# Attention beside a long convolution on one core: the score banks regrouped into a ring of six, with narrower convolution chunks and more probability slots

## The chip, the core and the metric

The kernel runs on one core of a Trainium2 chip. The metric is the device time of one execution in microseconds (us); before the change it is 903.99 us, the median of five runs (902.03 to 904.02). The engines are named as the profile names them: PE (TensorE, matmuls; PEld is its weight loads), ACT (ScalarE), DVE (VectorE), POOL (GpSimd) and SP (the queue that issues most DMAs). PSUM, into which PE writes and from which ACT and DVE read, has eight banks of 128 partitions x 512 fp32 numbers.

## What is computed

Two independent operators on 2048 positions and 640 channels, whose results stand side by side in the output. Shortened:

```python
# A: gated long convolution, one filter of 2048 taps for each channel
k_shift = sum(k_pad[:, t:t+S] * shift_k[:, 3-t] for t in range(4))
kv = k_shift * v
y  = irfft(rfft(kv, 2S) * rfft(ssm_k, 2S))[:S]      # causal convolution
a  = q * (y + kv * ssm_D)
# B: attention, 32 heads of 20 channels, no mask
q, k, v = split(x @ wqkv)
p = softmax(q @ k.T * 20**-0.5)                      # 32 x 2048 x 2048
b = (p @ v) @ wo
out = concat([a, b], -1)
```

The exponentials of B are 32 x 2048 x 2048 numbers. The convolution of A is done without an FFT, by matmuls with Toeplitz blocks of the filters.

## The kernel before, in words

**Attention.** Queries are taken in 4 chunks of 512 (qc), heads in 8 groups of 4 (g), keys in 16 blocks of 128 (kb): 512 blocks. A block has four *units*, one for each head: scores of 128 keys x 512 queries, which fill one PSUM bank. There are 2048 units. `S_task` (L209, matmul at L567) writes the scores of a group of units, one unit to a bank; `EXP_task` (L579, instruction at L584) lets ACT take the exponential of two or three neighbouring banks in one instruction and write them as bf16 into slots of `P_sb`; `PV_task` (matmul at L645) multiplies the four probability tiles of a block by V and sums them over the 16 key blocks in bank 6. V carries a column of ones, so that the softmax denominators come out of the same matmul.

**Exponentials on VectorE.** Some units are given to DVE: `VEXP_task` (L589) and `vexp_iter` do the exponential in five instructions (L614, L617, L619, L622, L624), of which only the first reads the bank. `vec_at` (L1061) decides whether a unit goes there. It refuses while two such units are in work, while DVE's planned work reaches more than 0.4 us past the present (L1063), while none of 4 slots (`NPV`) is free, while the preparation or the output steps of A are behind their pace (L1067 to L1071), and while the convolution has done fewer tiles than 40 x (n - 480) / 1488 at unit n (L1072).

**Banks.** After the first units, the groups alternate between three units in banks 0 to 2 and two units in banks 3 and 4 (`group`, L188). Bank 5 (`AUX`) takes the units for DVE and the side tasks, bank 6 the output of PV, bank 7 (`MISC`) the convolution.

**Side tasks** go through `mbank` (L354), which gives them bank 5 while the convolution runs: K and Q projections of 512 positions (`KQ_task`, matmul at L393, cast at L381), V projections (L448, L454), normalisation of finished heads (`N_task`, L669 to L677), transposes of the normalised output (L702) and the output projection (L719), each evacuated by DVE.

**Operator A.** `kv_iter` (L474) makes kv on DVE (L477, L507) and writes it and four shifted copies to DRAM. Then `conv_setup` and `conv_iter` (L847) run 40 tiles of 16 channels; each has 128 matmuls (L868) into bank 7, two DVE steps on the result (L881, L882), four more matmuls (L889) and one DVE cast (L895). The shifted kv comes in chunks of `CH` = 128 channels (`kvx_load`, 4 DMAs for each chunk), the filters in 160 sets of four DMAs, four sets ahead. After each chunk `A_iter` (L906) loads q and kv, does 12 DVE steps of 128 x 4 x CH (L912) and stores.

**Order.** Nothing is scheduled by hardware or compiler: a planner in the kernel (L1077 to L1166) builds the program in order. It keeps an estimated time for each engine, and at each step issues, by preference: a score group whose banks are free; a side task whose due time is near; PV of two blocks; a piece of convolution that fits into the time until ACT would run dry; a side task that is not yet due; or a pair of matmuls on zeros (`zeros`, L318) that keeps PE at work. DVE's steps of a unit go ahead of those of A (`dve_step`, L1006). All engines run their lists in order, with waits on semaphores. Loads of filters, loads and stores of A are all in SP's one list.

The parts of one SBUF region R are used first for loading and for kv, then for the convolution.

Of the kernel before, what the change touches and what calls it, by code (L numbers as in the profile page):

```python
# [24 lines left out]
NHK = 4  # L25
CH = 128
NPA, NPV = 25, 4
NPU = NPA + NPV
NQS = 9
NU = NB * 4  # L30
NPAIR = 40
KVPACE, CONV0, CONVE = 0.9, 480, 40

# [180 lines left out]
def build_kernel(nc, A_q, A_k, A_v, A_shift_k, A_ssm_k, A_ssm_D, B_x, B_wqkv, B_wo, out):  # L214
# [3 lines left out]
    with ExitStack() as es:  # L218
# [29 lines left out]

        HK_E, KVX_E, Y_E, AST_E = HKW, 64 * CH, 16 * CH, 4 * CH
        ph0 = NCC * 2 * D + 4 * 4 * D + 2 * 5 * D + 2 * KS * D + D + 2 * D  # L250
        ph1 = NHK * HK_E + 2 * KVX_E + 2 * Y_E + 4 * AST_E
# [12 lines left out]
        kst = [carve(5 * D).rearrange("p (j d) -> p j d", j=5) for _ in range(2)]  # L264
        Ctile = carve(KS * D).rearrange("p (j d) -> p j d", j=KS)
        tA = carve(D)
        tB = carve(KS * D).rearrange("p (j d) -> p j d", j=KS)
        kvst = [carve(D) for _ in range(2)]
# [11 lines left out]
        bkb = [Buf() for _ in range(8)]  # L280
        AUX, OBANK, MISC = 5, 6, 7

        kext = nc.dram_tensor("kext_scratch", (D, KXL), BF16).ap()
# [70 lines left out]
        def mbank():  # L354
            return min(mbanks(), key=lambda i: P.ready("pe", (), [bkb[i]]))

        def mbanks():
            return [AUX] + [MISC] * (not conv_on[0]) + [OBANK] * (pv[0] == 0) + [4] * (nu[0] < NPAIR - 4)

        pv, nu, conv_on = [0], [0], [0]  # L360

# [23 lines left out]

        def KQ_mm(which, g, bk, x0, n):
            off = g * 4 * DH
            Wt = WQ if which == "Q" else WKV

            def pe(e):  # L390
                for cc in range(NCC):
                    for i in range(4):
                        ins = e.matmul(bank[bk][32 * i:32 * i + DH, 0:n],  # L393
                                       Wt[:, cc, off + i * DH:off + (i + 1) * DH], xT[:, cc, x0:x0 + n],
                                       start=(cc == 0), stop=(cc == NCC - 1), tile_position=(0, 32 * i))
                return ins
            P.op("pe", pe, reads=b_xT[x0 // 128:(x0 + n + 127) // 128] + [b_W(g, which)], writes=[bkb[bk]],
                 c=0.02 + 1.08 * n / 512, st=1.06 * n / 512, kind="col")
# [30 lines left out]
        def qs(qc, g):  # L429
            return (qc * NG + g) % NQS  # L430

        def KQ_task(which, g, c):
# [41 lines left out]
        def kv_iter():  # L474
# [4 lines left out]
            for i in range(2):  # L479

                yield [RB(b_xst[2 + i])]
                assert all(("X", t) in done for t in range(8, NKB))
                b_KM.append(Buf(b_xst[2 + i]))
                P.op("dve", lambda e, i=i: e.memset(KM[i], 0.0), writes=[b_KM[i]], c=0.8)
# [30 lines left out]
        def setup_pool():  # L515
            P.op("pool", lambda e: e.memset(V_sb[:, :, :, DH:DH + 1], 1.0), writes=[b_ones])
            P.op("pool", lambda e: e.memset(kst[0][0:KS - 1, 0:KS, :], 0.0), writes=[b_kst[0]])
            P.op("pool", lambda e: e.memset(tB[:, 0, :], 0.0), writes=[b_tB])
            P.dma("sp", kst[1][:, 0:4, :], ap(A_shift_k, [[0, 128], [1, KS * D]]), d_sk, writes=[b_kst[1]])
            P.op("pool", lambda e: e.dma_start(  # L520
                ap(kext, [[5 * KXL, 128], [KXL, 5], [1, KPAD]]),
                ap(tB, [list(tB.ap[0]), [KPAD, 5], [1, KPAD]])), reads=[b_tB], writes=[b_kext], dsem=d_kext,
                extra=[t_x3])
            P.op("pool", lambda e: e.dma_start(
                ap(kext, [[KXL, D], [1, S]], KPAD), ap(A_ssm_k, [[S, D], [1, S]])), writes=[b_kext], dsem=d_kext, kb=2560)
            P.dma("sp", Wo_sb, ap(B_wo, [[D, 128], [128 * D, NCC], [1, D]]), d_small, writes=[b_Wo])
            P.dma("sp", Dbc, ap(A_ssm_D, [[0, 128], [1, D]]), d_small, writes=[b_D])
            kst_load(0)
# [9 lines left out]

        def group():

            n = nu[0]
            k, b0 = (2, 2 * (flip[0] % 2)) if n < NPAIR else (2, 3) if flip[0] % 2 else (3, 0)
            if n == NPAIR:
                rank[0] += -rank[0] % 5
            if rank[0] % NPA + k > NPA:
                rank[0] += 1
            return n, min(k, NU - n), b0
# [8 lines left out]
        def S_bufs(n, banks):  # L556
            rd = []
            for i in range(n, n + len(banks)):
                qc, g, kb = qgk(i // 4)
                rd += [x for x in (b_KT[(g, kb // 4)], b_QT[qs(qc, g)]) if x not in rd]  # L560
            return rd, [bkb[b] for b in banks]
# [253 lines left out]
        def conv_setup():  # L815
            xw = [b_WK0, b_Wa, b_Wb] + b_x0
            allx = xw + b_xst + b_KM + b_kst + [b_C, b_tA, b_tB] + b_kvst
            cv["HK"] = [Buf(*xw) for _ in range(NHK)]
            cv["KVX"] = [[Buf(*allx) for _ in range(4)] for _ in range(2)]
            cv["Y"] = [Buf(*allx) for _ in range(2)]  # L820
            cv["Aq"] = [Buf(*allx) for _ in range(2)]
            cv["Akv"] = [Buf(*allx) for _ in range(2)]
            cv["Z"] = [Buf(), Buf()]
            hk_load(0)
            for X in range(4):
                kvx_load(0, X)
            for qd in range(1, NHK):
                hk_load(qd)
# [113 lines left out]
        def deps(key):  # L942
            k = key[0]
            if k in "KQ":
                return [("X", t) for t in range(4 * key[2], 4 * key[2] + 4)]
            if k == "V":
                return [("X", key[1])]
            if k == "T":
                return [("O", key[1] - 1, key[2], hf) for hf in range(2)] if key[1] else []
            if k == "O":  # L950
                return [("T", key[1], key[2])]
            if k == "N" and key[2] == 0 and key[1]:
                return [("T", key[1] - 1, qt) for qt in range(4)]
            return []
# [12 lines left out]
        def reads_of(key):  # L967
            k = key[0]
            if k == "X":
                return [b_x(key[1])]  # L970
            if k in "KQ":
                return b_xT[4 * key[2]:4 * key[2] + 4] + [b_W(key[1], k)] + (
                    [RB(b_QT[qs(key[2], key[1])])] if k == "Q" else [])
            if k == "V":
# [11 lines left out]
        for g in range(NG):  # L986
# [4 lines left out]
            for qc in range(1, 4):  # L991
                add(128 * qc + 16 * g - 30, 1.24, ("Q", g, qc), lambda g=g, qc=qc: KQ_task("Q", g, qc),
                    (128 * qc + 16 * g - 16 * NQS + 16) * 4)
        for kb in range(NKB):
# [44 lines left out]
        def pick(limit, slack, now, bnow):  # L1039

            mg = 0.08 if bnow < 24 else -0.1
            free = min(P.ready("pe", (), [bkb[i]]) for i in mbanks()) <= now + mg
            for ent in sorted(pend):
                if ent[0] > limit:
                    return None
                if not free or ent[5] > nu[0] or any(k not in done for k in deps(ent[3])):
                    continue
                if ent[2] > slack and ent[0] > bnow + 2:
                    continue
                if P.ready("pe", reads_of(ent[3])) <= now + 0.08:  # L1050
                    return ent
            return None

        def pv_ready(b, now):
# [6 lines left out]
        def vec_at(n, now):  # L1061

            if len(chain) > 1 or not 140 < n < NU - 30 or P.T["dve"] > now + 0.4:  # L1063
                return False
            if owner[NPA + vn[0] % NPV] // 4 >= pv[0] or any(k not in done for k in S_needs(n, 1)):
                return False
            if not kv_over:  # L1067
                if kv_done[0] < (now - 60) * KVPACE:
                    return False
            elif micro and kv_done[0] < a_at[0] + 12 * (now - a_at[1]) / (20 if conv_over else 60):  # L1070
                return False  # L1071
            elif not conv_over and conv_b < 40 * (n - CONV0) / (NU - CONVE - CONV0):  # L1072
                return False
            rd, wr = S_bufs(n, [AUX])
            return P.ready("pe", rd, wr) <= now + 0.03

        while nu[0] < NU or pv[0] < NB - 1:  # L1077
# [10 lines left out]
            if nu[0] < NU:  # L1088
                n, k, b0 = group()
                while max(owner[rank[0] % NPA:rank[0] % NPA + k]) // 4 >= pv[0]:  # L1090
# [8 lines left out]
                if not need and P.ready("pe", rd, wr) <= now + 0.03:  # L1099
                    vec = vec_at(n + k, now)  # L1100
                    S_task(n, banks)
                    EXP_task(n, k, b0)
                    if vec:
                        S_task(n + k, [AUX])
                        VEXP_task(n + k, AUX)
                    exp_end.append(P.T["act"])
                    continue
# [6 lines left out]

            ent = pick(bnow + 6, slack, now, bnow)
            if ent:
# [39 lines left out]
            if sum(x[1] for x in P.stream) < 2.1 and slack > 0.45 and bnow > 1:  # L1156
# [3 lines left out]
                if P.ready("pe", (), [bkb[OBANK]]) <= now - 0.1:  # L1160
                    zeros(OBANK, 2, True)
                    continue
                if not tail[0] and P.ready("pe", (), [bkb[AUX]]) <= now - 0.1:
                    zeros(AUX, 2, True)
                    continue
# [79 lines left out]
```

## Time and profile before

| what | us |
|---|---|
| median of 5 runs | 903.99 |
| profiled execution, its own time | 904.02 |
| its span, first to last instruction | 902.2 |
| ACT busy | 883.3 |
| PE busy, ends modelled | 866.6 |
| DVE busy | 606.3 |
| POOL busy | 51.6 |
| convolution matmuls (L868), first to last | about 230 to 855 |

The share of the span that an engine is busy does not say that it sets the time: PE's matmuls overlap each other, and their ends are modelled. The chain that ended last says which work the end waited for. An instruction's duration is from its start to its end; where an engine starts the next one before the last has ended, the durations add up to more than the engine's busy time. "Idle before" is how long an engine had nothing to do just before an instruction, and the releaser is what ended that. Windows give the same for a stretch of the span.

### The profile page before, as it was taken

The numbers are of one execution on the slowest core, as the hardware profiler recorded it, in microseconds if no ns is written. First come the engines' busy times: TensorE is split into PE (matmuls) and PEld (weight loads), VectorE is DVE, ScalarE is ACT, GpSimd is POOL, SyncE is SP. The second block draws the span as 40 slices with busy tenths as digits, with TensorE's granted clock in tenths as the row PEclk, the third lists the DMA queues.
The fourth block names the chain that finished last, engine by engine and source line by source line (L and its number), as shares of the span: only waits on it lengthen the run. The fifth ranks groups of instructions, "written<-read, shape, count | busy, mean of one in ns | idle before, by whom it ended". The sixth has DMA issues, their size and how long they took to land.

```text
span 902.2 us, 26133 instructions
## 1 busy us (share of the span) xinstructions
PE 866.6 (96%) x11614; PEld 405.6 (45%) x11614; DVE 606.3 (67%) x1101; ACT 883.3 (98%) x789; POOL 51.6 (6%) x75
## 2 busy tenths in 40 slices
PE   9999999999999999999999999999999999999997
PEld 4433322222455544545455444544444555455422
DVE  3477776676667677776775777775676675776751
ACT  6999999999999999999999999999999999999996
POOL 3002133321000000000000000000000000000000
PEclk9999999999999999999999999999999999999899
DMA  9525367757767555887546967455884657664311
GB/s 295 163 71 158 95 202 235 208 135 162 186 165 199 159 156 126 192 195 186 151 121 183 209 164 195 127 152 134 204 222 122 168 140 191 177 182 138 82 42 35
DMA packets 131740, 144.97 MB, mean 161 GB/s; under 512 B 94993, under 2 KB 106379, under 8 KB 131627
## 3 DMA queue, kind: packets, MB, share of 16 engines
q1 hardware_dynamic: 120251, 129.60, 54.0%
q0 software_dynamic: 9920, 13.33, 5.6%
q8 instruction: 91, 1.49, 0.7%
q10 hardware_dynamic: 1456, 0.37, 0.2%
q14 instruction: 22, 0.18, 0.1%
HBM read 124.67 MB, written 21.09 MB: 162 GB/s over the span
## 4 chain that ended last, share of the span: by engine, by line
ACT 94%; PE 6%; DVE 0%; issue 0%; DVEq 0%
ACT P_sb L584 94%; PE PS L567 1%; PE PS L393 1%; PE PS L318 1%; PE PS L645 1%; PE PS L448 1%; PE PS L748 0%; PE PS L369 0%; PE PS L868 0%; DVE P_sb L792 0%; DVE OT_sb L654 0%; DVEq L1181 0%; PE PS L771 0%; PE PS L669 0%; DVE KT L381 0%
## 5 line engine op out<-in xcount | busy, mean ns | idle before, releaser
L584 ACT ACTIVATE P_sb<-PS 128x1024 bf16<-128x1024 f32 (+2 forms) x781 | 878.8, 1424 | 4.5 <-PE PS L567 4.3
L567 PE MATMUL PS<-QT,KT 20*128 20x512 bf16 x2048 | 304.4, 385 | 27.0 <-ACT P_sb L584 21.5
L868 PE MATMUL PS<-R 128*128 128x128 bf16 (+15 forms) x5120 | 250.4, 193 | 1.7 <-DVE R L895 1.7
L868 PEld LDWEIGHTS PS<-R 128*128 128x128 bf16 x5120 | 199.5, 96 | 106.1 <-issue 105.9
L567 PEld LDWEIGHTS PS<-QT,KT 20*128 20x128 bf16 x2048 | 74.8, 91 | 220.3 <-ACT P_sb L584 167.6
L645 PE MATMUL PS<-P_sb,V_sb 128*21 128x512 bf16 x2048 | 158.5, 384 | 1.5 <-DVE P_sb L624 1.2
L614 DVE TENSOR_SCALAR XI<-PS 128x512 int32<-128x512 f32 x107 | 74.0, 691 | 99.5 <-PE PS L567 99.5
L617 DVE SCALAR_TENSOR_TENSOR XZ<-XI 128x512 f32<-128x512 uint16 x107 | 73.8, 689 | 2.7
L624 DVE SCALAR_TENSOR_TENSOR P_sb<-XZ,XI 128x512 uint16<-128x512 f32 x107 | 73.6, 687 | 2.1
L619 DVE SCALAR_TENSOR_TENSOR XZ<-XZ,XI 128x512 f32<-128x512 f32 x107 | 73.5, 687 | 2.0
L318 PE MATMUL PS<-Zt 128*128 128x512 bf16 x230 | 69.3, 396 | 1.0 <-DVE Zt L312 1.0
L477 DVE TENSOR_TENSOR R<-R 128x640 bf16<-128x640 bf16 (+1 forms) x96 | 57.7, 601 | 1.6
L645 PEld LDWEIGHTS PS<-P_sb,V_sb 128*21 128x21 bf16 x2048 | 31.2, 89 | 58.9 <-issue 46.4
L654 DVE CAST OT_sb<-PS 128x512 bf16<-128x512 f32 x32 | 22.1, 690 | 45.4 <-PE PS L645 45.1
L192 POOL DMA_DIRECT2D kvm_scratch<-R x64 | 43.8, 690 | 139.9 <-DVE R L507 134.6
L622 DVE TENSOR_SCALAR XI<-XI 128x512 int16<-128x512 int16 x107 | 49.1, 459 | 2.5
L393 PE MATMUL PS<-xT,R 128*20 128x512 bf16 (+2 forms) x660 | 40.4, 374 | 0.0
L381 DVE CAST KT<-PS 128x512 bf16<-128x512 f32 (+1 forms) x32 | 21.7, 677 | 27.8 <-PE PS L393 27.8
L393 PE MATMUL PS<-xT,WQ 128*20 128x512 bf16 (+1 forms) x660 | 40.3, 374 | 0.0
L381 DVE CAST QT<-PS 128x512 bf16<-128x512 f32 (+1 forms) x32 | 21.9, 683 | 21.6 <-PE PS L393 21.6
L895 DVE CAST R<-PS 128x256 bf16<-128x256 f32 x40 | 17.0, 424 | 20.0 <-PE PS L889 18.7
L454 DVE CAST V_sb<-PS 128x160 bf16<-128x160 f32 (+1 forms) x48 | 18.3, 382 | 17.6 <-PE PS L448 17.1
(51 smaller groups left out, 352.4 us busy)
## 6 DMA issues: line engine op xcount, KB each, us to landing
R<-kext_scratch SPq DMA_DIRECT2D x640, 132.0 KB, 3.0
kvm_scratch<-R POOLq DMA_DIRECT2D x64, 160.0 KB, 5.3
R<-kvm_scratch SPq DMA_DIRECT2D x20, 512.0 KB, 5.5
R<-in_A_k_dram SPq DMA_DIRECT2D x15, 640.0 KB, 3.8
kext_scratch<-in_A_ssm_k_dram POOLq DMA_DIRECT2D x1, 2560.0 KB, 13.5
R<-in_A_v_dram SPq DMA_DIRECT2D x16, 160.0 KB, 4.2
kv_scratch<-R SPq DMA_DIRECT2D x16, 160.0 KB, 4.5
R<-in_A_q_dram SPq DMA_DIRECT2D x20, 128.0 KB, 2.6
```

The costliest lines, as they stand in the source:

```text
L318: P.op("pe", lambda e: e.matmul(bank[bk], Zt, zrhs, start=start, stop=start, skip_group_check=True), reads=[b_Zt], writes=[bkb[bk]], tok=s ...
L393: ins = e.matmul(bank[bk][32 * i:32 * i + DH, 0:n], Wt[:, cc, off + i * DH:off + (i + 1) * DH], xT[:, cc, x0:x0 + n], start=(cc == 0), sto ...
L477: P.op("dve", lambda e: e.tensor_tensor(o, a, b, op), reads=reads, writes=writes, c=c)
L567: ins = e.matmul(bank[b], KT[32 * u:32 * u + DH, g, kb * 128:(kb + 1) * 128], QT[32 * u:32 * u + DH, qs(qc, g), :], start=True, stop=True, ...
L584: P.op("act", lambda e: e.activation(P_sb[:, s0:s0 + k, :], PS[:, b0 * 512:(b0 + k) * 512].rearrange("p (u q) -> p u q", u=k), ACT.Exp, sc ...
L614: step(lambda e: e.tensor_scalar(XI, bank[bk], scale * 1.4426950408889634 * w, 127.0 * w, op0=ALU.mult, op1=ALU.add), [bkb[bk]], [bi])
L617: step(lambda e: e.scalar_tensor_tensor(XZ, u, w * c2 / c3, u, op0=ALU.add, op1=ALU.mult), [bi], [bz])
L619: step(lambda e: e.scalar_tensor_tensor(XZ, XZ, w * w * c1 / c3, u, op0=ALU.add, op1=ALU.mult), [bi, bz], [bz])
L622: step(lambda e: e.tensor_scalar(hi, hi, 128.0, None, op0=ALU.mult), [bi], [bi])
L624: step(lambda e: e.scalar_tensor_tensor(P_sb[:, slot[n], :].bitcast(U16), XZ, 128.0 * c3 / w ** 3, hi, op0=ALU.mult, op1=ALU.add), [bi, bz ...
L645: ins = e.matmul(bank[OBANK][32 * u:32 * u + DH + 1, :], V_sb[:, kb, 4 * g + u, :], P_sb[:, slot[4 * b + u], :], start=(kb == 0), stop=(kb ...
L868: P.op("pe", lambda e, o=o, lhsT=lhsT, rhs=rhs, st=st, last=last: e.matmul(o, lhsT, rhs, start=st, stop=last, skip_group_check=True), read ...
```

## The change

The six banks 0 to 5 become one ring of two groups of three, once the convolution runs. The third bank of a group (2 or 5) can be left out of the group and *lent* to a side task that is due within `SIDE` = 8 blocks, or its unit can go to DVE in place of ACT; then ACT takes two banks in that group. Before the convolution begins and in the last 40 units the old grouping (three and two) stays. The unit for DVE is now the third of its own group, where it had been one more unit in bank 5.

`vec_at` refuses only when DVE's planned work reaches 0.8 us past the present, where it was 0.4. The pace of `A_iter` for its refusals is 12 steps in 50 us, where it was 60. Q projections for the query chunks 1 to 3 become two halves of 256 positions into the two halves of one bank, which is held in between, with one cast. A chunk has 80 channels in place of 128, so there are 8 chunks in place of 5, with 5 tiles in each. There are 35 slots of P for ACT in place of 25; their room comes from the narrower chunk buffers and from putting two buffers of `kv_iter` (`Ctile`, `tB`) where the input x was staged.

The core of the diff:

```diff
-CH = 128
-NPA, NPV = 25, 4
+CH = 80
+NPA, NPV = 35, 4
+SIDE = 8
...
-        Ctile = carve(KS * D).rearrange("p (j d) -> p j d", j=KS)
+        Ctile, tB = xst[0], xst[1]
...
+        THIRD = (2, 5)
...
         def mbank():
-            return min(mbanks(), key=lambda i: P.ready("pe", (), [bkb[i]]))
+            bk = min(mbanks() or [i for i in THIRD if i not in held], key=lambda i: P.ready("pe", (), [bkb[i]]))
+            if bk == lent[0]:
+                lent[0] = 0
+            return bk
         def mbanks():
-            return [AUX] + [MISC] * (not conv_on[0]) + [OBANK] * (pv[0] == 0) + [4] * (nu[0] < NPAIR - 4)
+            if conv_on[0]:
+                return [lent[0]] if lent[0] else []
+            return [AUX] * (AUX not in held) + [MISC] * (MISC not in held) + [OBANK] * (pv[0] == 0) + [4] * (nu[0] < NPAIR - 4)
...
+        def Q_part(g, c, i):
+            if i == 0:
+                q_bank[(g, c)] = bk = mbank()
+                held.add(bk)
+                KQ_mm("Q", g, bk, c * 512, 256)
+            else:
+                bk = q_bank[(g, c)]
+                held.discard(bk)
+                KQ_mm("Q", g, bk, c * 512 + 256, 256, 256)
+                copy("dve", QT[:, qs(c, g), :], bank[bk], bkb[bk], b_QT[qs(c, g)], 0.7)
...
-        def group():
+        def group(now):
             n = nu[0]
-            k, b0 = (2, 2 * (flip[0] % 2)) if n < NPAIR else (2, 3) if flip[0] % 2 else (3, 0)
+            k, b0 = (2, 2 * (flip[0] % 2)) if n < NPAIR else (3, 3 * (flip[0] % 2))
+            if k == 3 and (b0 + 2 == lent[0] or b0 + 2 in held or b0 == 3 and (not conv_on[0] or n > NU - 40) or
+                           P.ready("pe", (), [bkb[b0 + 2]]) > now + 0.03):
+                k = 2
...
-            if len(chain) > 1 or not 140 < n < NU - 30 or P.T["dve"] > now + 0.4:
+            if len(chain) > 1 or not 140 < n < NU - 30 or P.T["dve"] > now + 0.8:
                 return False
...
-            elif micro and kv_done[0] < a_at[0] + 12 * (now - a_at[1]) / (20 if conv_over else 60):
+            elif micro and kv_done[0] < a_at[0] + 12 * (now - a_at[1]) / (20 if conv_over else 50):
...
-                    vec = vec_at(n + k, now)
-                    S_task(n, banks)
-                    EXP_task(n, k, b0)
-                    if vec:
-                        S_task(n + k, [AUX])
-                        VEXP_task(n + k, AUX)
+                    if conv_on[0]:
+                        if k == 3 and not lent[0] and side_due(bnow, now):
+                            k, lent[0] = 2, b0 + 2
+                        vec = k == 3 and vec_at(n + 2, now)
+                        S_task(n, banks[:k])
+                        EXP_task(n, k - vec, b0)
+                        if vec:
+                            VEXP_task(n + 2, b0 + 2)
+                    else:
+                        vec = vec_at(n + k, now)
+                        S_task(n, banks)
+                        EXP_task(n, k, b0)
+                        if vec:
+                            S_task(n + k, [AUX])
+                            VEXP_task(n + k, AUX)
```

`side_due` looks for a waiting side task, other than a second half of Q, that is due within 8 blocks and whose inputs will be there within 0.5 us. While a bank is lent or held, the planner looks at all waiting side tasks, and no longer only at those due within 6 blocks.

## The prediction

> **What bounds it now.** The page's busy shares and its chain that ended last were read first.
>
> ```profile
> PE 866.6 (96%) x11614; PEld 405.6 (45%) x11614; DVE 606.3 (67%) x1101; ACT 883.3 (98%) x789; POOL 51.6 (6%) x75
> ...
> ACT 94%; PE 6%; DVE 0%; issue 0%; DVEq 0%
> ```
>
> ACT is busy for 98% of the span and carries 94% of the chain; PE's 6% lies in the first 40 us and at the end. So the time goes down by what is taken from ACT, as long as nothing makes ACT wait. Next, ACT's groups of instructions with their shapes kept apart:
>
> ```profile
> L584 ACT ACTIVATE P_sb<-PS 128x1536 bf16<-128x1536 f32 x380 | 626.1, 1648 | 3.0 <-PE PS L567 2.8
> L584 ACT ACTIVATE P_sb<-PS 128x1024 bf16<-128x1024 f32 x400 | 482.7, 1212 | 1.5 <-PE PS L567 1.4
> ```
>
> ACT hardly idles (4.5 us). Its two prices follow. One bank: 1648 - 1212 = 436 ns. The two rows add to 1108.8 us, but the page has L584 busy for 878.8 us, so instructions overlap. The 781 instructions took 3 x 380 + 2 x 400 + 1 = 1941 banks; 1941 x 0.436 = 846.3 us, and the other 32.5 us are 0.042 us for each instruction. The remaining 107 of the 2048 units were done by DVE. **So one more unit on DVE is worth 0.436 us, one instruction less 0.042 us.**
>
> How many more can DVE take? The convolution stretch, 230 to 855 us, first as a window (PE, PEld, DVE, ACT, POOL, clock, DMA share), then its DVE groups:
>
> ```profile
> 230.00:855.00 625.00, 608.25 (x8946) 316.19 (x8943) 437.45 (x791) 624.71 (x554) 0.00 (x0) 1.00 0.64 165
> ```
>
> ```profile
> L614 DVE TENSOR_SCALAR XI<-PS 128x512 int32<-128x512 f32 x101 | 69.8, 691 | 94.7 <-PE PS L567 94.7
> L624 DVE SCALAR_TENSOR_TENSOR P_sb<-XZ,XI 128x512 uint16<-128x512 f32 x101 | 69.4, 687 | 1.9
> L617 DVE SCALAR_TENSOR_TENSOR XZ<-XI 128x512 f32<-128x512 uint16 x100 | 69.0, 690 | 2.6
> L619 DVE SCALAR_TENSOR_TENSOR XZ<-XZ,XI 128x512 f32<-128x512 f32 x100 | 68.7, 687 | 1.9
> L622 DVE TENSOR_SCALAR XI<-XI 128x512 int16<-128x512 int16 x100 | 45.9, 459 | 2.3
> L881 DVE CAST ZH<-PS 128x256 bf16<-128x256 f32 x40 | 16.8, 419 | 8.1 <-PE PS L868 7.8
> ...
> L895 DVE CAST R<-PS 128x256 bf16<-128x256 f32 x39 | 16.5, 424 | 16.7 <-PE PS L889 15.4
> ...
> L912 DVE TENSOR_TENSOR R<-R 128x512 bf16<-128x512 bf16 x32 | 13.5, 422 | 0.7
> ```
>
> 101 of the 107 units lie here. A unit is five steps: 69.8 + 69.4 + 69.0 + 68.7 + 45.9 = 322.8 us, or 3.2 us each. DVE is idle for 625 - 437.5 = 187.5 us, and half of it, 94.7 us, stands before L614, waiting for score matmuls: 0.94 us at each unit. The refusal at 0.4 us (L1063) explains it: a unit is admitted only when DVE is nearly dry, and its scores take PE at least one score matmul more.
>
> **The change, part by part.** *Admission at 0.8 us.* DVE then still has up to one step (0.69 us) to do while the scores are made. From below, none of the 94.7 us is saved; from above, all of it, 94.7 / 3.2 = 30 units. I take three quarters, 71 us, because the row names this one wait at every unit, while other work must be lined up for it to close.
>
> *Eight chunks for five.* Before, 48 steps L912 lie in the stretch (32 of the row shown, 16 with Dbc). After, seven chunks in place of four end in it: 84 steps. Were a step still 0.42 us, that is 15 us more; if it shrinks along the line between the 128x512 and the 128x640 tensor-tensor rows (423 and 488 ns), a 320-wide step is 0.33 us and the cost 7 us. To this come three more starts of `A_iter`, in which new units are refused until loads land (the 6.7 us that DVE waited for kv_scratch fell on 3 occasions; I allow 2 us each). I take 11 + 6 = 17 us, nearer the middle as neither width is in the trace. So 71 - 17 = 54 us, 17 units. Outside the stretch I add one (205 to 230 us: DVE idle 8 of 25 us). **18 units x 0.436 = 7.8 us.** Bounds: -21 / 3.2 = -7 units in the stretch if nothing of the wait is saved and chunks cost 15 + 6 us, +30 - 2 = +28 with all of it and 7 us.
>
> *Groups of three.* Before, the stretch has 554 ACT instructions of 2.5 banks, 1385. After, 1385 - 17 = 1368 banks. Groups of two are those with a DVE unit (118) and those that lend a bank. Side tasks in the stretch, by their evacuations: 18 Q, 23 head normalisations, 12 transposes, 24 projections, 77; each shortens one or two groups, since the bank comes back only after DVE's cast, and I take 1.3, 100 groups. Then 218 groups of two take 436 banks, (1368 - 436) / 3 = 311 of three the rest: 529, 25 less. **25 x 0.042 = 1.0 us** (1.4 us at one group each, 0.3 us at two). [...]
>
> [...]
>
> *Score matmuls and PE.* A lent bank or a DVE unit adds no score matmul. Q in halves makes 40 matmuls for 20: halves of 256 appear as 40 in 1.3 us against 20 of 512 in 1.19 us, +0.1 us on 18 tiles. PE hides it: between 250 and 850 us it waited 91 us for ACT to free score banks (81.7 in its weight loads, 9.3 in matmuls), besides its matmuls on zeros. If that cover were gone it would cost 2 us.
>
> *A new wait.* Score matmuls into banks 2 and 5 now also wait for DVE's reading of a unit or a side task. Queued behind them on PE are PV and convolution; ACT waits for the group. The planner takes two banks if the third is not due free, so it arises only where DVE runs later than planned; the cover is the group ACT is in, 1.3 us (3 x 0.436 + 0.042), longer than a DVE step. Zero, at most one 0.69 us step at a few tens of units, some 10 us, which the upper end takes in with the slower rival.
>
> *DMA.* Rows of 160 B for 256 B, the same bytes: chunk loads go from 20 x 2048 to 32 x 2048 packets, loads and stores of A from 60 x 512 to 96 x 512, 43,000 more. Between 550 and 600 us, without a chunk change, DMAs are 54% busy at 141 GB/s; between 500 and 550 us, with one, 78% at 187. So 0.24 x 50 us x 16 engines for 8192 chunk packets and a few of A, some 23 ns each; 43,000 of them are 62 us of all 16 engines, and the stretch goes from 64% to about 74%. The sets for four quads ahead hide that: nothing. The packets of one chunk change are as many as before, so its peak is no higher.
>
> [...]
>
> *35 slots, shared buffers.* More slots let PV lag, and take no instruction away: nothing. `Ctile` and `tB` wait for the first x tiles' transposes, which come before those that the same step waited for already; SP's and POOL's lists keep their order there: nothing. SP's list grows by 12 chunk loads and 36 transfers of A; its long waits in 250 to 850 us are for PE to free filter sets (183 us), so issuing has room.
>
> Sum: 904.02 (span 902.2, and 1.8 around it; the runs' median is 903.99) - 7.8 - 1.0 = **895.2 us**.
>
> **The rivals.** *Unit count unchanged.* The other refusals (A's pace, two units in work) take over from 0.4 us. For it: DVE also waits for many short things beside L614. Only the groups remain: 904 - 1 = 903.0 us.
>
> *Slower: the convolution's own pace.* The stretch does 1385 + 101 = 1486 units in 40 tiles, 37.2 units a tile, exactly the pace of L1072 (1488 / 40). A DVE that is always full makes the two returns in each tile, L881 and L895, wait; before they found it idle (8.1 and 16.7 us). One step of 0.69 us at each is 2 x 0.69 x 40 = 55 us. If PE cannot use its windows meanwhile, tiles fall behind and L1072 refuses units until DVE is emptier by those 55 us: 17 fewer than before, 904 + 7.4 - 1.0 = 910.4 us. It decides as soon as a tile lasts over 37.2 units. Against it: PE waits for ACT 91 us in that stretch and could catch up, and longer groups give longer windows.
>
> *More.* The whole wait closes, and part of DVE's other 93 us of idle time: +40 units, 904 - 17.4 - 1 = 885.6 us.
>
> **How the numbers follow.** Chances: forecast 0.55, unchanged 0.13, slower 0.2, more 0.12. A run can tell about 0.2%, 1.8 us, from no change. Faster: 0.55 + 0.12 and a little of the unchanged case, 0.70; same 0.10; slower 0.20. The range reaches from just below the case of more, 885, to near the slower one, 908; the bounds of the forecast itself, 890 (28 + 1 units, 1.4 us) to 906 (7 - 1 lost, 0.3 us), lie inside.
>
> **What would show it.** Right: about 125 instructions at L614, the idle time before each well under 0.5 us, DVE busy over 70% in the stretch, some 750 instructions at L584 with the 1536-wide the majority in the stretch, and ACT's idle time still about 5 us. Wrong: L614 at 107 or less, or L868 reaching past 880 us (pace); ACT idle by tens of us before L584 with PE waiting for DVE at L567 (the new wait); PE waiting for R<-kvm_scratch (DMA).

## The result, and the profile after

The change runs at **902.09 us** (median of 53 runs, 900.83 to 908.0) against 903.94 us for the kernel before (95 runs, 901.24 to 919.01): a ratio of 0.9976, 95% interval 0.9966 to 0.9986. Ratios, here and below, leave out the few runs that were more than 1.5% above the fastest of their kernel; medians do not. The change is faster, but by 0.24% where I had forecast 1%. The 895.2 us are 7 us away; the rival "unit count unchanged", 903.0 us, is nearest. The profiled execution of after took 907.72 us (span 905.9), more than most of its runs. A *dip* explains that, a stretch in which the granted clock of TensorE is 0.50; it lies at 230 us and is shown below.

The page of after, first busy shares, then the granted clock in 40 slices, then the chain:

```profile
PE 873.2 (96%) x12174; PEld 422.3 (47%) x12174; DVE 605.2 (67%) x1127; ACT 883.7 (98%) x761; POOL 51.6 (6%) x75
...
PEclk9999999999699999999999999999999999999999
...
ACT 89%; PE 7%; DMA 2%; DVE 1%; SPq 0%; issue 0%; POOL 0%; POOLq 0%; DVEq 0%
```

ACT sets the end as before, and DVE is no busier (605.2 us, was 606.3). ACT's groups by shape, now at L610:

```profile
L610 ACT ACTIVATE P_sb<-PS 128x1536 bf16<-128x1536 f32 x437 | 643.5, 1639 | 6.2 <-PE PS L593 5.9
L610 ACT ACTIVATE P_sb<-PS 128x1024 bf16<-128x1024 f32 x316 | 350.3, 1201 | 2.6 <-PE PS L593 2.5
```

437 and 316 are 753 instructions where there were 781. They took 3 x 437 + 2 x 316 = 1943 banks, so DVE did 2048 - 1943 = 105 units. Before it did 107. The groups came out as forecast; the units did not: 18 more were forecast, and two fewer came.

The convolution stretch, 230 to 860 us as it now lies (PE, PEld, DVE, ACT, POOL, clock, DMA share, GB/s), and DVE's groups in it:

```profile
230.00:860.00 630.00, 615.68 (x9211) 324.94 (x9208) 428.35 (x801) 625.05 (x526) 0.00 (x0) 0.99 0.70 164
```

```profile
L640 DVE TENSOR_SCALAR XI<-PS 128x512 int32<-128x512 f32 x96 | 66.3, 690 | 55.0 <-PE PS L593 54.0
...
L938 DVE TENSOR_TENSOR R<-R 128x320 bf16<-128x320 bf16 x56 | 18.0, 322 | 1.3
...
L921 DVE CAST R<-PS 128x256 bf16<-128x256 f32 x38 | 16.1, 424 | 23.8 <-PE PS L915 23.5
L907 DVE CAST ZH<-PS 128x256 bf16<-128x256 f32 x38 | 16.1, 423 | 43.6 <-PE PS L894 43.5
...
L740 DVE CAST Bout<-PS 128x320 bf16<-128x320 f32 x24 | 11.8, 491 | 23.2 <-PE PS L745 23.2
L388 DVE CAST QT<-PS 128x512 bf16<-128x512 f32 x17 | 11.8, 691 | 21.8 <-PE PS L400 21.6
```

L640 is the old L614, and the wait before it did shrink: 55.0 us for 96 units, 0.57 us each, where it was 94.7 for 101, 0.94 each. **But DVE is idle for 630 - 428.35 = 201.7 us, more than the 187.5 before.** The 40 us that closed there reappeared at other rows: the cast of a convolution tile (L907) waits 43.6 us where it waited 8.1, the output projection's cast (L740) 23.2 for 6.7, the Q cast (L388) 21.8 for 10.6. A wait in an in-order list is closed only if the list gets something else to do at that point; here it did not.

### The profile page after: what moved, and what is told of

Read it like the earlier page. It is cut to its first block, busy times and chain, and to the rows that moved or that the text cites. A ratio compares the mean times of both kernels' runs of the same rounds, so it can differ in the third digit from the quotient of the medians.

```text
span 905.9 us, 27478 instructions
## 1 busy us (share of the span) xinstructions
PE 873.2 (96%) x12174; PEld 422.3 (47%) x12174; DVE 605.2 (67%) x1127; ACT 883.7 (98%) x761; POOL 51.6 (6%) x75
## 4 chain that ended last, share of the span: by engine, by line
ACT 89%; PE 7%; DMA 2%; DVE 1%; SPq 0%; issue 0%; POOL 0%; POOLq 0%; DVEq 0%
ACT P_sb L610 89%; PE PS L593 2%; PE PS L400 1%; PE PS L671 1%; PE PS L894 1%; DMA kvm_scratch<-R 1%; DMA R<-kvm_scratch 1%; PE PS L319 1%; PE PS L774 0%; DVE R L498 0%; SPq L193 0%; PE PS L469 0%; PE PS L376 0%; POOL kvm_scratch L193 0%; DVE P_sb L818 0%
## 5 line engine op out<-in xcount | busy, mean ns | idle before, releaser
L610 ACT ACTIVATE P_sb<-PS 128x1536 bf16<-128x1536 f32 (+1 forms) x753 | 879.2, 1455 | 8.7 <-PE PS L593 8.3
L593 PE MATMUL PS<-QT,KT 20*128 20x512 bf16 x2048 | 294.2, 387 | 23.8 <-ACT P_sb L610 18.5
L894 PE MATMUL PS<-R 128*128 128x128 bf16 (+15 forms) x5120 | 252.5, 194 | 3.1 <-DMA R<-kvm_scratch 1.7
L894 PEld LDWEIGHTS PS<-R 128*128 128x128 bf16 x5120 | 202.7, 97 | 105.0 <-issue 103.8
L593 PEld LDWEIGHTS PS<-QT,KT 20*128 20x128 bf16 x2048 | 72.5, 91 | 210.2 <-ACT P_sb L610 163.4
L640 DVE TENSOR_SCALAR XI<-PS 128x512 int32<-128x512 f32 x105 | 72.5, 690 | 61.4 <-PE PS L593 60.4
L319 PE MATMUL PS<-Zt 128*128 128x512 bf16 x310 | 91.1, 388 | 1.5 <-DVE Zt L313 1.0
L650 DVE SCALAR_TENSOR_TENSOR P_sb<-XZ,XI 128x512 uint16<-128x512 f32 x105 | 72.3, 689 | 2.4
L907 DVE CAST ZH<-PS 128x256 bf16<-128x256 f32 x40 | 16.9, 423 | 43.7 <-PE PS L894 43.5
L400 PE MATMUL PS<-xT,WQ 128*20 128x256 bf16 (+1 forms) x1140 | 43.2, 287 | 0.0
L388 DVE CAST QT<-PS 128x512 bf16<-128x512 f32 (+1 forms) x32 | 21.9, 683 | 31.8 <-PE PS L400 31.5
L388 DVE CAST KT<-PS 128x512 bf16<-128x512 f32 (+1 forms) x32 | 21.7, 677 | 24.8 <-PE PS L400 24.6
L319 PEld LDWEIGHTS PS<-Zt 128*128 128x128 bf16 x310 | 21.0, 98 | 28.8 <-issue 22.0
```

The source lines that it names most:

```text
L319: P.op("pe", lambda e: e.matmul(bank[bk], Zt, zrhs, start=start, stop=start, skip_group_check=True), reads=[b_Zt], writes=[bkb[bk]], tok=s ...
L400: ins = e.matmul(bank[bk][32 * i:32 * i + DH, o:o + n], Wt[:, cc, off + i * DH:off + (i + 1) * DH], xT[:, cc, x0:x0 + n], start=(cc == 0), ...
L593: ins = e.matmul(bank[b], KT[32 * u:32 * u + DH, g, kb * 128:(kb + 1) * 128], QT[32 * u:32 * u + DH, qs(qc, g), :], start=True, stop=True, ...
L610: P.op("act", lambda e: e.activation(P_sb[:, s0:s0 + k, :], PS[:, b0 * 512:(b0 + k) * 512].rearrange("p (u q) -> p u q", u=k), ACT.Exp, sc ...
L640: step(lambda e: e.tensor_scalar(XI, bank[bk], scale * 1.4426950408889634 * w, 127.0 * w, op0=ALU.mult, op1=ALU.add), [bkb[bk]], [bi])
L650: step(lambda e: e.scalar_tensor_tensor(P_sb[:, slot[n], :].bitcast(U16), XZ, 128.0 * c3 / w ** 3, hi, op0=ALU.mult, op1=ALU.add), [bi, bz ...
```

## The experiments

"Units" below are the instructions of DVE's first step, out of 2048. The table has every kernel; the text takes them by question. Ratios are to the kernel before, measured beside each batch (its median was 902.29 us beside e1 to e4, 903.70 beside e5 to e8, 904.04 beside e9 to e12), with 95% intervals.

| kernel | median us | ratio | units |
|---|---|---|---|
| e1, before with 0.8 | 915.35 | 1.0091 (1.0057 to 1.0126) | 118 |
| e2, e1 with 80 channels | 912.42 | 1.0122 (1.0090 to 1.0154) | 113 |
| e3, after without the ring | 918.04 | 1.0161 (1.0128 to 1.0195) | 109 |
| e4, after with 25 slots | 925.60 | 1.0245 (1.0208 to 1.0283) | 104 |
| e5, e3 with filling zeros | 904.90 | 1.0001 (0.9975 to 1.0027) | 109 |
| e6, e5 with pace 300 | 945.05 | 1.0458 (1.0429 to 1.0487) | 120 |
| e7, e6 with 0.6 and whole Q | 942.03 | 1.0430 (1.0396 to 1.0464) | 122 |
| e8, after with 0.4 | 907.60 | 1.0047 (1.0018 to 1.0076) | 97 |
| e9, after with filling zeros | 904.00 | 0.9981 (0.9953 to 1.0009) | 105 |
| e10, e9 with all of A's loads ahead, pace 100, 0.6 | 899.72 | 0.9926 (0.9897 to 0.9955) | 113 |
| e11, e10 without the ring, whole Q | 899.64 | 0.9938 (0.9910 to 0.9965) | 116 |
| e12, after with 0.85 | 913.17 | 1.0080 (1.0045 to 1.0115) | 108 |

### One part alone: the admission, then the chunks

Theory: the later admission alone gives units, and other parts of the change take them back. Rival: the refusals beside it leave it none.

```diff
-P.T["dve"] > now + 0.4:
+P.T["dve"] > now + 0.8:
```

> The kernel before with only the admission at 0.8 us. Its list holds 118 DVE units, 11 more than before. The forecast's own theory (a unit is worth 0.436 us and nothing else changes): 11 x 0.436 = 4.8 us less, 899.2 us, ACT idle time still about 5 us, idle time before the first step of a unit well under 0.94 us each. The theory of a second limit (the units are there, but PE then runs late with scores or convolution): idle time before the unit's first step falls too, ACT idle time rises by about as much as the units take away, time within 3 us of before.

e2 is the same with `CH = 80`.

> The run before it, with chunks of 80 channels in addition. Its list holds 113 DVE units. If eight output stages cost DVE what the prediction said (17 us, 5 units): 5 x 0.436 = 2.2 us more than the run before it. If narrow rows hurt by DMA instead: PE waits for R<-kvm_scratch and convolution matmuls come later, 5 us or more.

e1 has 118 units, 11 more than before, and e2 113: the narrower chunks cost five, as I had priced them. **Both are slower all the same**, e1 by 0.9% where 11 x 0.436 = 4.8 us should have been won. The wait per unit did shrink, to 71.7 / 108 = 0.66 us, and in all by 94.7 - 71.7 = 23.0 us, which at 3.2 us are the 7 units more in this stretch (108 for 101). Three views of e1 show it and what took the gain: DVE's first step in 230 to 860 us, the PE timeline (start, length, line, idle before it and releaser), and three windows:

```profile
L614 DVE TENSOR_SCALAR XI<-PS 128x512 int32<-128x512 f32 x108 | 74.7, 692 | 71.7 <-PE PS L567 69.1
```

```profile
688.35 0.40 PE L645 MATMUL PS<-P_sb,V_sb 128*21 128x512 bf16 x4 [1.90 <-DVE P_sb L624]
```

```profile
680.00:690.00 10.00, 7.96 (x102) 3.91 (x102) 7.26 (x15) 9.08 (x9) 0.00 (x0) 1.00 0.72 169
690.00:702.00 12.00, 12.00 (x139) 6.77 (x127) 7.97 (x13) 8.89 (x8) 0.00 (x0) 0.50 0.34 91
702.00:710.00 8.00, 8.00 (x94) 3.66 (x92) 2.96 (x6) 7.30 (x7) 0.00 (x0) 0.90 0.47 137
```

A unit admitted while DVE still has 0.8 us to do is also finished later, and PV, which PE does in order, stands until it is there. Such waits of PE for L624 were 1.2 us in four places before; in e1 they are 10.7 us in eleven. After one of 1.90 us the granted clock drops to 0.50, until 703.7 us. PE is then busy for all of the 12 us shown, and ACT, fed at half speed, for 8.89 of them. The profile has two more such dips, of 3.4 us, at 232 and 253 us, after waits of 1.90 and 1.59 us for L624. ACT's waits for scores are 9.9 us where they were 4.3.

### The ring, and the dip at the start of the convolution

Theory: the ring is worth its 25 instructions, 1 us. Rival: it carries more, or costs units. e3 is after with the ring switched off (`RING = 0`: groups of three and two, bank 5 for side tasks and units); halves, slots, chunks and both planner numbers stay.

```diff
+RING = 0
...
+            if k == 3 and b0 == 3 and not RING:
+                k = 2
...
-                    if conv_on[0]:
+                    if RING and conv_on[0]:
```

> The changed kernel with the ring of six switched off: groups of three and two in banks 0 to 4, bank 5 for side tasks and DVE units, as before; the wide admission, 80 channels, 35 slots, Q in halves and the pace of 50 us stay. Its list holds 109 DVE units and 780 exp instructions where the changed kernel has 105 and 753. If the ring is where the change earns its time (prediction: 25 instructions less, 1 us): 1 us slower than the changed kernel or the same. If the ring itself costs DVE units and convolution time: the convolution ends tens of us earlier than in the changed kernel, and the time is equal or better.

It is 16 us slower than after, with 109 units, four more. The PE timeline at the start of the convolution and the windows around it:

```profile
227.26 0.39 PE L596 MATMUL PS<-QT,KT 20*128 20x512 bf16 x3
231.71 1.01 PE L897 MATMUL PS<-R 128*128 128x128 bf16 x9 [4.06 <-DMA R<-kvm_scratch]
```

```profile
225.00:231.00 6.00, 2.13 (x14) 0.60 (x13) 3.12 (x5) 4.46 (x4) 0.00 (x0) 1.00 1.05 167
231.00:240.00 9.00, 8.29 (x85) 4.24 (x85) 3.85 (x6) 4.39 (x4) 0.00 (x0) 0.51 0.81 196
240.00:260.00 20.00, 20.00 (x216) 9.71 (x220) 8.15 (x14) 13.94 (x12) 0.00 (x0) 0.50 0.44 103
```

PE stands 4.06 us for the first filters' kv, and the clock is 0.50 until 269 us. ACT is busy 22.8 of these 35 us. So e3 doesn't measure the ring. e5 is e3 with 14 matmuls on zeros ahead of the first convolution matmul, so that PE doesn't stand:

```diff
+if conv_b == 0 and 0 < pv[0] % NKB:
+    for _ in range(14):
+        P.op("pe", lambda e: e.matmul(bank[OBANK], Zt, zrhs, start=False, stop=False, skip_group_check=True),
+             reads=[b_Zt], writes=[bkb[OBANK]], tok=False, c=0.0, kind=P.kind)
```

> The kernel of the no-ring run with 14 matmuls on zeros put into PE's list just before the first convolution matmul, everything else in the same order. In the no-ring run PE stood 4.1 us for R<-kvm_scratch there and the granted clock was 0.50 from 231 to over 264 us while ACT waited. If the standing PE is what lowers the clock and the lower clock is what costs the time: no stretch at 0.50 near 230 us, ACT's idle time before exp down by 10 us or more, time 902 to 906 us. If the late data itself costs it: clock the same or not, time still 910 us or more.

```profile
225.00:231.00 6.00, 5.48 (x36) 2.35 (x32) 3.13 (x5) 4.31 (x4) 0.00 (x0) 1.00 1.18 212
231.00:240.00 9.00, 9.00 (x152) 4.88 (x150) 6.55 (x11) 8.31 (x8) 0.00 (x0) 1.00 0.71 178
240.00:260.00 20.00, 19.48 (x320) 10.64 (x318) 14.91 (x28) 20.00 (x19) 0.00 (x0) 1.00 0.61 155
```

The dip is gone in the profile, all 12 runs have a mean clock of 0.999 or 1.0, and the time falls from 918.04 to 904.9 us with the same work and units. **The dip cost about 13 us**: in e3's profile ACT stood for 13.5 of the 38 us from 231 to 269 us. After itself has a small one. The first two of these windows in after's profiled execution, and then in before's:

```profile
225.00:231.00 6.00, 3.85 (x48) 1.83 (x48) 2.12 (x4) 4.90 (x4) 0.00 (x0) 0.93 1.25 194
231.00:240.00 9.00, 9.00 (x99) 4.58 (x95) 6.26 (x10) 5.79 (x5) 0.00 (x0) 0.50 0.86 212
```

```profile
225.00:231.00 6.00, 5.55 (x65) 1.68 (x61) 4.00 (x8) 6.00 (x6) 0.00 (x0) 1.00 0.99 246
231.00:240.00 9.00, 9.00 (x157) 5.20 (x150) 6.55 (x11) 9.00 (x9) 0.00 (x0) 1.00 0.55 149
```

After's ACT loses 1.1 + 3.2 us here, before's nothing. But before's profiled execution has a dip of its own, near the end of the convolution:

```profile
850.00:875.00 25.00, 23.54 (x194) 7.63 (x193) 13.83 (x30) 23.15 (x21) 0.00 (x0) 0.86 0.16 37
```

From 852.3 to 859.1 us the clock is 0.50, and ACT loses 25 - 23.15 = 1.85 us. PE's longest stand in the 7 us ahead of it is 0.44 us, so it needs no long wait. The 904.02 us that the prediction started from had this dip in it.

Is the dip at 230 us where the missing 7 us went? e9 is after with the same filling.

> The changed kernel with the 14 matmuls on zeros before the first convolution matmul, all else in the same order. In the changed kernel's profile PE stood for late data at 228 us and the clock was 0.50 for 12 us. If that dip is all that the changed kernel loses to the clock: clock 1.0 throughout, runs closer together, median 901 to 902 us; it is then bound by its list of 105 units and 753 exp instructions and not by the clock. If the change's missing 7 us lay in the clock: 895 to 898 us.

It is not. e9's clock is 1.0 in 11 of 12 runs, and it takes 904.0 us. Of the 56 executions of after whose clock is on record, 40 have 0.999 or 1.0, with medians of 901.5 and 901.9: the dip is in few of them, and the zeros cost about 2 us. Against e5 (904.9), which differs by the ring alone, e9 is 0.9 us faster, though the two intervals overlap. The list doesn't explain that: 27 instructions fewer at 0.042 us and 4 units fewer at 0.436 us would make it 0.6 us slower.

The dips differ in what lies ahead of them and in their length. PE had stood 1.90 us at one time ahead of e1's dip at 690 us, e3's began within the stand of 4.06 us, and in the 7 us ahead of before's at 852 us PE stood no more than 0.44 us at a time; the clock was at 0.50 for 13.7 us in e1, 37.6 us in e3 and 6.83 us in before, with PE busy by the records.

### The slots

I had put the 35 slots at nothing. e4 is after with `NPA = 25`.

> The changed kernel with 25 slots of P in place of 35, nothing else. Its list holds 104 DVE units and the same number of exp instructions within 2. The prediction priced the slots at nothing: 902 to 903 us. The rival: in a ring of threes fewer slots force PV ahead of the scores, ACT waits for scores by some 10 us: 910 to 914 us, and ACT's idle time shows it.

It is the largest loss of any single part: 925.6 us with 104 units, one fewer than after. The longest relevant rows of its waits (engine, line, releaser: us, times, longest):

```profile
ACT P_sb L610 <- PE PS L593: 26.9, 38, 2.3
...
PEld PS L671 <- DVE P_sb L650: 14.2, 20, 2.5
PE PS L671 <- DVE P_sb L650: 8.9, 11, 2.4
```

It is the wait of e1 again. After has no wait of PE's matmuls on L650, and its weight loads wait 0.5 us in two places. That fits PV lagging behind ACT until DVE's unit is done with 35 slots, and coming too early with 25. The clock then falls (a mean of 0.964 in the profiled run): of its five dips ahead of the last instructions, three (at 372, 536 and 577 us, ACT idle for 9.1 us in them) follow waits for L650, while those at 232 and 901 us (8.2 us) follow short stands of at most 0.63 us, mostly for ACT. So the slots are needed in this list; that PV's wait is the whole of their worth isn't shown.

### The admission, once the rest is in place

e8 and e12 are after with 0.4 and 0.85 in place of 0.8.

> The changed kernel with the admission back at 0.4 us. Its list holds 97 DVE units, 8 fewer than the changed kernel, with about the same number of exp instructions. If admission is worth what the prediction said for each unit: 8 x 0.436 = 3.5 us slower than the changed kernel, 905.6 us, idle time before a unit's first step back near 0.9 us each. If admission brings nothing inside the ring: 902 us.

```profile
L640 DVE TENSOR_SCALAR XI<-PS 128x512 int32<-128x512 f32 x91 | 62.9, 691 | 82.4 <-PE PS L593 82.4
```

The wait at each unit is back to 82.4 / 91 = 0.91 us, and there are 97 units, 8 fewer. At a clock of 1.0, e8 takes 905.4 us (6 runs), after 901.9 (32 runs): 3.5 us for 8 units, 0.44 each. The price of a unit was right.

> The changed kernel with the admission at 0.85 us in place of 0.8, nothing else. Its list holds 108 DVE units, 3 more. By price alone: 1.3 us less than the changed kernel, 900.8 us. If the planner's order, and not the number of units, decides at this scale: some other time, up to 5 us slower, with ACT's lateness and not its work making the difference.

```profile
ACT P_sb L610 <- PE PS L593: 17.6, 22, 2.4
...
PEld PS L671 <- DVE P_sb L650: 6.9, 4, 2.6
PE PS L671 <- DVE P_sb L650: 5.8, 3, 2.3
...
PE PS L894 <- DMA R<-kext_scratch: 3.4, 2, 2.8
```

Three more units and 11 us slower. New are three waits of PE's matmuls for L650, up to 2.3 us, one of 2.8 us for filters (kext_scratch), and three stretches of 25 us with a mean clock of 0.80 to 0.86 (from 425, 575 and 700 us), in which ACT is busy for 60.9 of 75 us. The dips of the first and the third follow a wait for L650, that of the second the wait for filters. At 0.8 the order that the planner writes happens to have no such waits; at 0.85 it has. How much of after's gain is such luck of one order I can't tell from two settings.

### What refuses the units: A's pace

e8 shows that units bring their price, and after has two fewer than before. So what refuses them? e6 is e5 with the pace of A's steps set from 50 to 300 us for 12, which nearly removes that refusal; e7 does the same with whole Q tiles and 0.6.

> The run before it with the pace in the refusal for A's output steps at 12 steps in 300 us in place of 50. Its list holds 120 DVE units, 11 more than the run before it. If A's pace is what held the units back, and ACT still waits for nothing: 11 x 0.436 = 4.8 us less than the run before it, 897 to 901 us. If the DVE is then so full that PV waits for its units (as in the run with the wide admission alone): stretches at clock 0.50 in the middle of the span, 905 us or more.

> No ring, whole Q projections of 512 as before the change, admission at 0.6 us, pace 300 us, the 14 matmuls on zeros, 80 channels and 35 slots kept. Its list holds 122 DVE units and about 775 exp instructions. At 0.436 us for each of 15 units more than before the change: 902.3 - 6.5 = 895.8 us, if no stretch at clock 0.50 comes in. If DVE's fullness makes PE stand: 903 us or more, as in the run with the wide admission alone.

Eleven and thirteen more units than e5, and 40 and 37 us slower. The rows of e6's waits that have grown against e5:

```profile
DVE R L941 <- DMA R<-kv_scratch: 52.9, 21, 4.2
ACT P_sb L819 <- PE PS L777: 50.8, 1, 50.8
...
PE PS L698 <- DVE OT_sb L683: 43.6, 1, 43.6
```

Without the pace, A's steps are put off to the end: 18 of the 21 waits for loads of kv lie after 860 us, one after the other, and before its last instructions ACT waits 50.8 us for the output projection (4.3 us in e5), which stands behind DVE. So the pace does hold units back, and it is there for a reason. e10 gives A what it needs to be late without a tail: four buffers, with all of a chunk's loads issued at its start, and a pace of 100 us; admission is 0.6, with e9's filling.

```diff
-Aq = [... for _ in range(2)]
-Akv = [... for _ in range(2)]
+Aq = [... for _ in range(4)]
+Akv = [... for _ in range(4)]
...
-            A_load(B, 0)
-            A_load(B, 1)
+            for h in range(4):
+                A_load(B, h)
...
```

> The run before it with four buffers in place of two for the output stage of A, so that all its loads are issued at its start, the pace of its refusal at 12 steps in 100 us and the admission at 0.6 us. Its list holds 113 DVE units, 8 more than the changed kernel, 753 exp instructions as there. If refusals for A withheld units, and units are worth 0.436 us: 8 x 0.436 = 3.5 us less than the run before it, 897.5 to 899 us. If steps of A pile up at the end as with the pace of 300 us: over 905 us, with PE waiting for DVE in the last 40 us.

**899.72 us, 113 units.** Its interval (0.9897 to 0.9955) lies below that of after: it beats both kernels, and at a clock of 1.0 as well (899.2 us against 901.9 and 902.2). Against e9, 8 units x 0.436 = 3.5 us were expected and 4.3 came. Its page, and the two DVE groups in 230 to 860 us that changed places in after:

```profile
PE 866.3 (96%) x12174; PEld 422.3 (47%) x12174; DVE 628.0 (70%) x1167; ACT 879.1 (98%) x760; POOL 51.6 (6%) x75
```

```profile
L640 DVE TENSOR_SCALAR XI<-PS 128x512 int32<-128x512 f32 x106 | 73.2, 691 | 61.5 <-PE PS L593 60.3
...
L907 DVE CAST ZH<-PS 128x256 bf16<-128x256 f32 x39 | 16.4, 420 | 13.3 <-PE PS L894 12.7
```

The wait at a unit is 61.5 / 106 = 0.58 us, the same as in after, while the wait at L907 is 13.3 us instead of 43.6. DVE is busy 628.0 - 605.2 = 22.8 us more than in after, most of the 25.6 us that eight units take: with these refusals eased, idle time that had moved to other rows, to L907 above all, was filled by units.

Last, e11: e10 without the ring and with whole Q.

> No ring, whole Q projections, the four output buffers, pace 100 us, admission 0.6 us, the matmuls on zeros. Its list holds 116 DVE units and about 778 exp instructions. By price: 9 units and about 3 instructions better than before the change, 9 x 0.436 + 0.1 = 4.0 us less than before, 898 us. If the ring is worth more than its instructions, it falls behind the run before it.

899.64 us, the same as e10. It has 116 units, three more (3 x 0.436 = 1.3 us), and 777 exponentials on ACT, 25 more (25 x 0.042 = 1.1 us): the ring's shorter list is paid for with units. With whole Q and no ring the same time is reached.

## Why the prediction was wrong

**The prices were right.** In the traces the time from the start of one L610 (or L584) to the next, where ACT isn't kept waiting, is 0.904 us for two banks and 1.330 for three: 0.426 for a bank and 0.052 for an instruction, where I had 0.436 and 0.042. (I had spread all 878.8 us of busy time over banks and instructions; 1941 x 0.426 + 781 x 0.052 = 867.5, and the rest is late starts.) At these prices after should gain 28 x 0.052 - 2 x 0.426 = 0.6 us. Where the clock is 1.0, before takes 902.2 us (median of 25 of the 70 runs beside the experiments) and after 901.9 (32 runs), 0.2 to 0.3 us less. The rest of the 1.85 us between the medians goes with the clock: of before's 95 runs 29 lie under 902.5 us, 37 between 903.4 and 904.1 (beside the experiments the clock of such runs is 0.996), and 16 over 909, while 38 of after's 53 lie under 902.7. The dip at 852 us in before's profile, 1.85 us, has the size of the step from the first of these groups to the second. So the measured gain is mostly that after has dips less often (the clock is 1.0 in 32 of its 56 executions, and in 25 of those 70 of before). The prediction says nothing of that, and that the rival with an unchanged unit count lies so near is in good part luck.

**Groups of three: right.** 28 instructions fewer, 25 forecast.

**The failed step is "I take three quarters, 71 us", and the 18 units that follow from it.** I took the wait before L614 as time that units would fill once the refusal at 0.4 us was relaxed. With that edit alone (e1) 23.0 us of it closed, a third of the 71; with the whole change 40 us did, while waits at other rows grew by more. A unit has to pass all refusals, and the others stayed. The runs give the staircase: 107 units before, 118 with 0.8 alone, 113 with eight chunks, 109 with the slots, halves and the pace of 50 us, 105 with the ring. The admission's own part was thus 11 (I had 22 in the stretch, where 7 came), the chunks took the 5 that I had given them, and 8 more went with parts that I had charged no unit. I had named this as the first rival, "the other refusals take over", and gave it 0.13. That A's pace is one of them is shown by e6, which changed it alone; e10 changed buffers, pace and admission at once. How the last 8 units divide between A's pace, halves, slots and the ring stays open, and so does which refusal held the units that e1 didn't get.

**Chunks: right.** Of the two prices for a 320-wide step the one on the line between two rows, 0.33 us, holds: L938 takes 0.322. The five units that I took off for the chunks are the difference between e1 and e2.

**A new wait: wrong in place and in price.** I looked for PE waiting for banks 2 and 5 and priced it at ACT's wait alone. Where the change's parts were tried without the rest (e1, e2, e4), the wait came in PV, for the probabilities of DVE's unit, and with it the clock fell: after a stand of 1.90 us e1 ran at half speed for 13.7 us. Before has no such wait of PE's matmuls over 0.4 us, and after has none. But neither is free of dips, as their profiles show at 852 and 230 us, and e8, with the late admission of before, has a clock below 0.997 in 6 of 12 runs. So PV's wait is one way into a dip, not the only one.

**"35 slots: nothing" failed** by 23 us (e4 against after), in the company of the ring and 0.8 us.

**Slower, the convolution's pace: partly there.** I had named "L868 reaching past 880 us" as its sign, and L894, its new line, runs until 879.6 us where L868 ended at 854.4. ACT's last L610 starts at 895.8, and no 17 units were lost. The tiles are later with the ring (876.2 us in e9, 840.2 in e5 without it) and with the later admission (859.4 in e8 with 0.4); e10, with most units of the kernels with the ring, ends them at 861.7. So a late convolution is no fixed price of the ring; what in the list makes it late wasn't taken apart.

**DMA: right in the main.** 43,776 packets more in the first queue, 43,000 forecast, and a share of 0.70 in the stretch, up by 0.06 where 0.10 was forecast. The "nothing" needs one exception: the first filters' kv arrives 1.7 us late for PE, and in the profiled run the dip at 230 us comes just after. **Q in halves**: 960 matmuls of 256 positions in place of 480 of 512. I had PE's idle time hide them; no run has the halves alone.

## What to carry to other kernels

A wait in the profile belongs to the rule that caused it only until that rule is relaxed: list every rule that can refuse, and count for each how often it would, before the idle time is priced as work. Where an engine's clock falls after it has stood, as PE's does here, price a new wait of 2 us not at 2 us but with the slow stretch after it (in e1 13.7 us at 0.50 came after 1.90 us of standing), and look for it at every consumer of the delayed result. Before two kernels are compared to 0.2%, compare their runs at the same clock. And test a part in the company of the others: the slots, worth nothing by count, carried the later admission.

## What the runs showed of the hardware

The granted clock of TensorE fell to 0.50 for 6.83 us in before (at 852 us) and for 13.65 us in after (at 230 us): two and four steps of 3.41 us. In both profiles the clock falls once more after the last instruction, 15 and 198 whole steps after the first fall. The profiles of before, after, e1, e2, e3, e4 and e12 have 19 dips ahead of the last instructions. As far as the windows tell, to about 0.3 us, each lasts a whole number of such steps (1 in e1 at 232 us, 4 in e1 at 690, 11 in e3 at 231).

In the step ahead of the dip PE had stood for 0.83 us in all in before (in pieces of at most 0.44 us), 1.69 us in after, 1.8 us in e1 (at 690 us) and all 3.41 us in e3 (at 231 us). No other step up to 896 us in before, and none up to 902 us in after, had more than 0.80 us. Why before's dip lasts two steps and e3's eleven, with PE busy by the records, stays open.

ACT, the engine that sets the time, was busy for 0.64 of the dip in e3 (231 to 269 us), 0.71 of it in after, 0.73 in before and 0.74 in e1 (8.89 of the first 12 us from 690 us). With 14 matmuls on zeros over such a place, 23 of 24 runs (e5 and e9) had a mean clock of 0.999 or 1.0. The times of the kernel before fall into steps by its mean granted clock: medians of 902.2 us at 1.0 (25 of the 70 runs beside the experiments), 903.9 at 0.996 (20), 905.4 at 0.992 (3) and 910.2 at 0.987 (15), with the same instructions in the same order.
